# Last chunk of a gated feed-forward: half of its token tiles by seven products, the chunks of the second half in another order

## The chip, the core and the metric

The kernel runs on one core of one Trainium2 chip. The metric is the time of one execution in microseconds on the device; the time before is the median of three runs. One more execution was taken with the hardware profiler, and all rows below come from it. PE is TensorE (PEld its weight loads), DVE is VectorE, ACT is ScalarE, POOL is GpSimd, SP is SyncE, which issues the DMAs.

## What is computed

One block of a model on 2048 tokens of width 576: a layer norm, a linear attention with 32 heads, and a gated feed-forward of width 4608, all in float32.

```python
x = A_x                                        # [2048, 576]
xn = layernorm(x)
s = linear_attention(xn, A_wqkv, A_wo)         # phi(q) (phi(k)^T v) / (phi(q) . z), then @ wo
h = gelu(xn @ B_w1 + B_b1)                     # [2048, 4608]
g = silu(h @ B_w2 + B_b2)                      # [2048, 576]
return x + s * g
```

## The kernel before

**Precision.** TensorE works in a fast float32 form with a short mantissa. So each operand is split into a high part (ScalarE casts it, `set_hi`) and a low part (VectorE subtracts, `set_lo`), and each product is three matmuls: high by high, high by low, low by high. A split costs ScalarE one instruction and VectorE one, and the low one has two operands in SBUF.

**Stages.** The first 280 us compute the layer norm, the state of the attention and `s`, which is kept in DRAM (`s_dram`). The feed-forward follows: two halves of 1024 tokens, and in each half nine chunks (`NC`) of 512 hidden units (`CF` = 4 blocks of 128). A step of the loop is one chunk of one half: two up projections (`Up`, seven products each), then the down projection.

**Seven products.** Up and down projections are done by a Strassen-Winograd scheme: a two-by-two block product in seven block products instead of eight, with sums of operands ahead and sums of results behind. In the down projection the token side is split into two blocks of 512 tokens (b = 0, 1) and the output side into two halves of 288 columns. A token tile is 128 tokens; tiles 0 to 3 are block 0, tiles 4 to 7 block 1. `product(c, i, q2, ...)` does product i for two tiles (q2 and q2 + 1) of the block: 12 matmuls of 288 columns into one pair of PSUM banks (`bank2`, three pairs in rotation), after which VectorE adds the result into `macc` in SBUF (line 1293). Products 2, 3 and 4 add into the banks in which 1, 5 and 7 were formed (`CHAIN`), so they start only when VectorE has read those. `macc` holds C11, C12, C21, C22 and U1; U1 is added to the last three at the end (`combine`, line 1303). Sums of the gelu outputs are formed on GpSimd in place (`HOps.S`), sums of w2 likewise, and the split operands of both weights are stored in DRAM in the first half and loaded back in the second (`W1Loaded`, `W2.load`).

**Order.** Within a chunk VectorE, ScalarE, GpSimd and TensorE run in program order (`in_order`). What runs beside the 14 up products and 14 down products of a step is put at one of `NS` = 28 places by tables (`PH`, `PW2`, `W2_NEXT`), through `add(base + place, ...)`. The DMA queue of SP is ordered by the scheduler.

**The last step** (chunk 8 of the second half) does not use seven products for the down projection. `W2.plain` cuts the raw w2 chunk into four blocks, each split high and low; `tail_split` and `tail_lo` split the eight gelu outputs; `down_plain` does each of the eight token tiles by 24 matmuls of 288 columns and finishes it at once: VectorE adds the PSUM result to `macc` (line 1398), ScalarE applies silu (line 1399), VectorE multiplies by `s` (line 1356) and adds `x` (line 1357, for tile 6 on GpSimd), and the tile is written out (line 1358). Tile 7 is done in two column parts, 384 and 192, so that its end is short. `load_xs` brings the `x` and `s` tiles into buffers that have become free.

Of the kernel before, what the change touches and what calls it, by code (L numbers as in the profile page):

```python
# [44 lines left out]
def linear_attention_gated_ffn(ctx, tc, x, xT, wqkv, wo, w1, w1e, b1, w2, b2, out):  # L45
# [619 lines left out]

    def load_w2_raw(n):
        raw = w2rp.tile([P, 4, CF // 2, HD], F32, tag="w2raw", name=f"w2raw{n}")
        nc.sync.dma_start(raw.rearrange("p b a d -> p (b a d)"), w2[n % NC])
        return raw
# [155 lines left out]
    def load_we(n):  # L825

        we_sb[n] = w1p.tile([P, WB, P], F32R, tag="we", name=f"we_{n}", bufs=2)
        dst = we_sb[n].bitcast(F32).rearrange("p b c -> p (b c)")
        g, q = divmod(n % NP, WG)
# [8 lines left out]
    class W1:  # L838


        def __init__(self, n):
            self.n = n
            raw = stage_w1(f"w1raw{n}")
            nc.sync.dma_start(raw, w1[n % NP])
# [43 lines left out]
    class W1Loaded(W1):  # L888


        def __init__(self, n):
            self.n, self.tiles = n, {}
            for i in ("a", "c", "d"):
                if i == "c":
                    t = w1r.tile([P, 8, P], F32R, tag="stw", name=f"wc_{n}")
                else:
                    t = w1_tile(i, n)
                self.tiles[i] = t
                nc.sync.dma_start(t.bitcast(F32), w1_dram[n % NP, i])

    def load_six(n):

        t = w1_tile("e", n)
        for k in range(2):
            six[n + k] = t[:, 4 * k : 4 * k + 4]
            nc.sync.dma_start(six[n + k].bitcast(F32), w1_dram[(n + k) % NP, 6])
# [223 lines left out]
    class Up:  # L1130


        def __init__(self, n, w, xs):
            self.p, self.w = n % NP, w
# [54 lines left out]
    class W2:  # L1189


        def __init__(self, n):
            self.n, self.ops, self.tiles = n, {}, {}
# [14 lines left out]
        def plain(self, f):  # L1208
            k = 2 - 2 * (f % 2)
            self.src["p", f] = self.raw[:, k : k + 2, f // 2]  # L1210

        def hi(self, i):
            tag = ORDER[i[1]] if isinstance(i, tuple) else i
            self.tiles[i], self.ops[i] = op_tile(fr, [2, HD], f"w2_{tag}", 1, f"w2_{self.n}_")
            set_hi(self.ops[i], self.src[i])

        def lo(self, i):
            set_lo(self.ops[i], self.src[i], nc.vector)
            if self.n < NC - 1:
                keep_op(w2_dram, (self.n, i), self.tiles[i])  # L1220

        def load(self, i):
            t, self.ops[i] = op_tile(fr, [2, HD], f"w2_{i}", 1, f"w2_{self.n}_")
            nc.sync.dma_start(t.bitcast(F32), w2_dram[self.n % NC, i])

    class HOps:
# [10 lines left out]

        def S(self, i, pr):
            A = lambda r, c: self.A[pr, r, c]
# [11 lines left out]
            else:  # L1251
                src[7, pr] = mid[:, 3 + pr]
                tt(src[7, pr], A(0, 0), A(1, 0), op=SUB)  # L1253

        def hi(self, i, pr):
            self.ops[i, pr] = hi_lo(gp, [P, 512], f"h{HBUF[i, pr]}", 1, f"h{i}{pr}_")
            set_hi(self.ops[i, pr], self.src[i, pr])

        def lo(self, i, pr):
            set_lo(self.ops[i, pr], self.src[i, pr], nc.vector)  # L1260

# [48 lines left out]
    def load_xs(t):  # L1310
        F = lambda v: v.bitcast(F32)
        flat = lambda v: F(v).rearrange("p a b -> p (a b)")[:, :D]
        if t == 0:
            xt, s_t = flat(w1_tile("a", "x0")), stage_w1("s0")[:, :D]
        elif t == 1:
            xt = flat(w1_tile("a", "x1"))
            s_t = flat(w1p.tile([P, WB, P], F32R, tag="we", name="s1", bufs=2))
        elif t == 2:
            xt, s_t = (flat(w1_tile("a", f"{v}2")) for v in "xs")
        elif t == 3:  # L1320
            xt, s_t = stage_w1("x3")[:, :D], flat(w1_tile("a", "s3"))
        elif t == 4:
            raw = F(fr.tile([P, 2, D], F32R, tag="w2_5", name="xs4", bufs=1))
            xt, s_t = raw[:, 0], raw[:, 1]
        else:
            if t == 5:
                tails["h"] = F(x_hi(2, "xs56")).rearrange("p a b -> p (a b)")
                tails["l"] = F(x_lo(2, "xs7")).rearrange("p a b -> p (a b)")
            v = {5: tails["h"], 6: tails["h"][:, 2 * D :], 7: tails["l"]}[t]
# [5 lines left out]
    def tail_split(b, f):  # L1335
        src = h.A[f // 2, b, f % 2]
        if b == 0:
            pair = hi_lo(gp, [P, 512], f"h{f}", 1, f"hp{f}_")
        else:
            k = f % 2  # L1340
            if f < 2 and ("t", 0) not in tails:
                tails["t", 0] = x_lo(0, "hp0")
            if f >= 2 and ("t", 1) not in tails:
                tails["t", 1] = x_lo(1, "hp1")
            t = tails["t", f // 2]
            pair = t[:, 2 * k, :], t[:, 2 * k + 1, :]
        set_hi(pair, src)
        tails["hs", b, f] = pair, src

    def tail_lo(b, f):  # L1350
        pair, src = tails["hs", b, f]
        set_lo(pair, src, nc.vector)

    def gate(t, c, xt, s_t, cs=slice(0, D), eng=nc.vector):

        nc.vector.tensor_tensor(s_t[:, cs], c[:, cs], s_t[:, cs], op=MUL)
        eng.tensor_tensor(s_t[:, cs], s_t[:, cs], xt[:, cs], op=ADD)
        nc.sync.dma_start(out[t * P : (t + 1) * P, cs], s_t[:, cs])

# [27 lines left out]
    def down_plain(t, ws):  # L1387

        bi, q = divmod(t, QH)
        cs = slice(q * P, (q + 1) * P)  # L1390
        seq = []
        for f, (wh, wl) in enumerate(ws):
            hh, hl = tails["hs", bi, f][0]
            seq += [(hh, wh), (hh, wl), (hl, wh)]
        dst = c_tile(bi, q).rearrange("p n d -> p (n d)")

        def end(ps, c):
            nc.vector.tensor_tensor(c, ps, c, op=ADD)
            nc.scalar.activation(c, c, AF.Silu)

        def mm(ps, w, i):
            st, w_all = seq[i]
            nc.tensor.matmul(  # L1403
                ps, st[:, cs], w_all.rearrange("p n d -> p (n d)")[:, w],
                start=(i == 0), stop=(i == len(seq) - 1),
            )

        if t < 7:
            ps = bank2(f"pd{t}")
            for i in range(len(seq)):  # L1410
                for h in range(2):
                    mm(ps[:, h, :HD], slice(h * HD, (h + 1) * HD), i)
            end(ps[:, :, :HD], as2(dst))
            gate(t, dst, *tails["xs", t], eng=nc.gpsimd if t == 6 else nc.vector)
            return

        parts = [slice(0, 384), slice(384, D)]
        ps = []
        for k, w in enumerate(parts):
            n = w.stop - w.start  # L1420
            ps.append(bank1(f"pd{t}_{k}")[:, :n])
            for i in range(len(seq)):
                mm(ps[k], w, i)
        for k, w in enumerate(parts):
            end(ps[k], dst[:, w])
        for w in parts:
            gate(t, dst, *tails["xs", t], cs=w)
# [62 lines left out]
    )  # L1490
    plans = {}
# [20 lines left out]
    for step in range(n_chunks):  # L1512
# [3 lines left out]
        h = HOps(c)  # L1516
# [23 lines left out]
        elif not plain:  # L1540
# [3 lines left out]
            if step + 2 < n_chunks:  # L1544
                make(W2, w2t, step + 1)
                for i, at in W2_NEXT.items():
                    add(base + at + 10 * change, lambda i=i, n=step + 1: w2t[n].load(i))
            else:
                make(W2, w2t, step + 1)
                add(base + 7, w2t[step + 1].load_raw)  # L1550
        if not plain:
# [8 lines left out]
            for what in ("S", "hi", "lo"):  # L1560
                for (i, pr), at in PH[what].items():
                    add(base + at, getattr(h, what), i, pr)
        else:
            for f in range(CF):
                w2t[step].plain(f)
                add(base + (1, 2, 3, 8)[f], w2t[step].hi, ("p", f))
                add(base + (2, 3, 8, 9)[f], w2t[step].lo, ("p", f))
# [14 lines left out]
        if plain:  # L1582
            for m in (C12, C21, C22):
                add(base + 4, combine, m, nc.gpsimd)
            for t, at in enumerate((6, 7, 12, 13, 5, 12, 12, 12)):
                add(base + at, load_xs, t)
            for b, f, at, lo in (
                (0, 0, 7, 8), (0, 1, 8, 9), (1, 0, 10, 10), (1, 1, 10, 11), (0, 2, 11, 12),
                (0, 3, 12, 13), (1, 3, 13, 13), (1, 2, 13, 13),
            ):  # L1590
                add(base + at, tail_split, b, f)
                add(base + lo, tail_lo, b, f)
# [66 lines left out]
```

## Time and profile before

| | |
|---|---|
| median of 3 runs | 1098.09 us (1097.7 to 1098.24) |
| profiled execution | 1098.02 us |
| its span, first to last instruction | 1096.3 us |
| around the span | 1.7 us |
| instructions | 18084 |
| first matmul of the last down projection | 1065.1 us |

Rows of a timeline give the start and the duration in us, the engine, the line of the kernel, the operation, the tile written and the tiles read, the shape and the count of merged instructions; in brackets the idle time before it and who ended it. A matmul row lasts longer than its place in the stream, since matmuls overlap: the distance from one start to the next is what counts. Rows by line give the least, median and largest duration in ns. Rows of windows give the busy time of an engine, its instructions, the clock granted to TensorE (1.00 is full), the busy share of the DMA engines and GB/s.

### The profile page before, as it was taken

Reading aid. Unit: us, or ns where it says so; the run is one execution under the profiler, and the core shown is the slowest. Engines: PE = TensorE matmul, PEld = TensorE weight load, DVE = VectorE, ACT = ScalarE, POOL = GpSimd, SP = SyncE. Lnnn points to the kernel's source line nnn. Section 1 sums busy time; section 2 is a strip of 40 time slices with the busy share of each in tenths; the row PEclk is TensorE's granted clock in tenths of the full one; section 3 lists DMA queues with packets and bytes.
Section 4 is the critical chain, followed back from the end, with each engine's and each line's share of the span. In section 5 each row is a group of like instructions: output and inputs, shape, how many; then the busy total and the mean of one; then the engine's idle time right before and its main releaser. Section 6 shows DMA issues by size and latency. Waiting matters only on the chain.

```text
span 1096.3 us, 18084 instructions
## 1 busy us (share of the span) xinstructions
PE 1088.6 (99%) x6702; PEld 1008.5 (92%) x6702; DVE 825.6 (75%) x1132; ACT 490.9 (45%) x844; POOL 472.7 (43%) x403
## 2 busy tenths in 40 slices
PE   9999999999999999999999999999999999999998
PEld 8999989999898998989989989899898998998987
DVE  7785748888798888888888888667476584664856
ACT  6454655555545354454453544524224233242352
POOL 4667444323546446464555553424234143242340
PEclk9999999999999999999999999999999999999999
DMA  7999834675959559486585779978676676766352
GB/s 248 269 262 280 311 135 160 205 242 188 342 214 344 190 211 332 152 317 233 187 330 167 287 239 405 387 249 296 210 245 217 204 236 217 229 222 228 122 181 87
DMA packets 88400, 262.54 MB, mean 239 GB/s; under 512 B 11894, under 2 KB 24182, under 8 KB 85624
## 3 DMA queue, kind: packets, MB, share of 16 engines
q1 hardware_dynamic: 88312, 261.38, 70.1%
q8 instruction: 53, 0.87, 0.3%
q14 instruction: 35, 0.29, 0.1%
HBM read 164.24 MB, written 95.17 MB: 237 GB/s over the span
## 4 chain that ended last, share of the span: by engine, by line
PE 99%; DVE 1%; issue 0%; POOL 0%; ACT 0%; DVEq 0%; POOLq 0%
PE pm L1287 35%; PE a L1148 10%; PE e L1148 10%; PE zy L1148 10%; PE pk L313 6%; PE pq L313 5%; PE ps_s L789 5%; PE b L1148 5%; PE pv L313 4%; PE pd L1403 2%; PE ps_kva L382 1%; PE ptp L771 1%; PE ps_kw L708 1%; PE warm L361 0%; PE ps_kvb L382 0%
## 5 line engine op out<-in xcount | busy, mean ns | idle before, releaser
L1293 DVE TENSOR_TENSOR macc<-pm,macc 128x576 f32<-128x576 f32 x218 | 163.8, 752 | 51.9 <-PE pm L1287 50.3
L813 ACT CAST h_h<-g 128x512 fp32r<-128x512 f32 x204 | 121.7, 621 | 133.9 <-PE pm L1287 132.8
L816 DVE TENSOR_TENSOR h_l<-g,h_h 128x512 fp32r<-128x512 f32 x204 | 161.7, 800 | 0.0
L1253 POOL TENSOR_TENSOR mid<-g 128x512 f32<-128x512 f32 x34 | 44.0, 1293 | 105.4 <-ACT g L1156 105.4
L1247 POOL TENSOR_TENSOR g<-g 128x512 f32<-128x512 f32 x34 | 54.9, 1615 | 49.4 <-DVE h_l L816 28.4
L1156 ACT ACTIVATE g<-b,b1c 128x512 f32<-128x512 f32 x36 | 24.8, 689 | 101.9 <-DVE b L1174 101.9
L1165 ACT COPY mid<-a 128x512 f32<-128x512 f32 x36 | 21.1, 585 | 96.4 <-PE a L1148 96.4
L859 POOL TENSOR_TENSOR w1raw<-w1raw 128x256 f32<-128x256 f32 x18 | 13.3, 737 | 116.7 <-ACT h_h L813 68.2
L1168 DVE TENSOR_TENSOR mid<-b,mid 128x512 f32<-128x512 f32 x36 | 24.8, 690 | 46.3 <-PE b L1148 43.0
L1375 POOL TENSOR_TENSOR fin1l<-fin1h,fin1l 128x288 f32<-128x288 f32 x8 | 6.4, 806 | 119.6 <-DMA fin1l<-s_dram 62.9
L1250 POOL TENSOR_TENSOR g<-g 128x512 f32<-128x512 f32 x34 | 55.2, 1623 | 2.7
L1148 PE MATMUL a<-h0r,wa 128*128 128x512 f32 x144 | 50.4, 390 | 0.0
L1148 PE MATMUL a<-xh,wa 128*128 128x512 f32 x144 | 50.4, 390 | 0.0
L816 DVE TENSOR_TENSOR h_l<-mid,h_h 128x512 fp32r<-128x512 f32 x34 | 48.8, 1437 | 1.2
L1156 ACT ACTIVATE g<-e,b1c 128x512 f32<-128x512 f32 x36 | 24.8, 689 | 51.5 <-DVE e L1181 51.5
L754 POOL TENSOR_TENSOR pbuf<-phiq,den 128x576 f32<-128x576 f32 x16 | 19.4, 1214 | 63.9 <-DVE den L753 63.9
L1244 POOL TENSOR_TENSOR g<-g 128x512 f32<-128x512 f32 x34 | 44.2, 1299 | 2.7
L1181 DVE TENSOR_TENSOR e<-e,mid 128x512 f32<-128x512 f32 x36 | 24.8, 689 | 21.5 <-PE e L1148 21.5
L1171 DVE TENSOR_TENSOR mid<-zy,mid 128x512 f32<-128x512 f32 x36 | 24.9, 691 | 19.5 <-PE zy L1148 19.5
L313 PE MATMUL pk<-wkv_h,xh 128*128 128x288 f32 (+1 forms) x160 | 38.1, 320 | 0.5 <-DVE xh L245 0.5
L313 PE MATMUL pk<-wkv_l,xh 128*128 128x288 f32 (+1 forms) x160 | 38.2, 321 | 0.0
L1174 DVE TENSOR_TENSOR b<-e,mid 128x512 f32<-128x512 f32 x36 | 25.2, 699 | 17.2 <-PE e L1148 16.2
(857 smaller groups left out, 3644.4 us busy)
## 6 DMA issues: line engine op xcount, KB each, us to landing
we<-we_dram SPq DMA_DIRECT2D x36, 448.0 KB
w2raw<-w SPq DMA_DIRECT2D x10, 1152.0 KB
op<-w2o SPq DMA_DIRECT2D x18, 576.0 KB
w1raw<-w SPq DMA_DIRECT2D x18, 512.0 KB
op_a<-wa SPq DMA_DIRECT2D x18, 512.0 KB
op_c<-wc SPq DMA_DIRECT2D x18, 512.0 KB
op_d<-wd SPq DMA_DIRECT2D x18, 512.0 KB
wc<-op_c SPq DMA_DIRECT2D x18, 512.0 KB
```

Source lines behind the costliest of these rows:

```text
L313: nc.tensor.matmul(ps[:, h, : ws.stop - ws.start], st, w[:, k, ws], start=(begin and i == 0), stop=(end and i == len(seq) - 1), skip_group ...
L789: nc.tensor.matmul(ps[:, h, :HD], st[:, k, :], w[:, k, h * HD : (h + 1) * HD], start=(i == 0), stop=(i == len(seq) - 1),)
L813: nc.scalar.copy(pair[0], src)
L816: eng.tensor_tensor(pair[1], src, pair[0].bitcast(F32), op=SUB)
L1148: nc.tensor.matmul(ps, st, mv, start=first and n == 0, stop=n == len(seq) - 1, skip_group_check=True,)
L1156: nc.scalar.activation(g, ps, AF.Gelu_apprx_tanh, bias=b1c[:, f : f + 1])
L1244: tt(src[5, pr], A(1, 0), A(1, 1), op=ADD)
L1247: tt(src[6, pr], src[5, pr], A(0, 0), op=SUB)
L1250: tt(src[3, pr], A(0, 1), src[6, pr], op=SUB)
L1253: tt(src[7, pr], A(0, 0), A(1, 0), op=SUB)
L1287: nc.tensor.matmul(ps[:, q, :HD], hs[p][st][:, cs], m[:, p, :], start=(n == 0 and i not in CHAIN), stop=(n == 5), skip_group_check=True,)
L1293: nc.vector.tensor_tensor(dst, src, dst, op=ADD)
```

## The change

In the second half the chunks are taken in the order 8, 0, 1, ..., 7 (`chunk`, `pair`). So the step after the change of halves uses the w2 operands of the chunk before it, which are still in SBUF, and loads none; and the last step works on chunk 7, whose seven w2 operands lie in DRAM, where chunk 8 had its raw weights loaded and split. One more block of w2, B01, is loaded raw and split (`load_b01`, `place_b01`).

In the last step the down projection of tiles 0, 1, 4 and 5 goes by seven products (`seventh`), 12 matmuls each; tiles 2, 3, 6 and 7 stay plain (`plain_tile`), 24 matmuls each. TensorE's order is: product 1, tile 2, products 2, 6, 7, 5, 4, 3, tiles 3, 6, 7. The sums and splits for the products are made on the 256 columns that they need (`LastHOps`, `PLAST`); most of them stand in the tail itself, between the products. U1 is added in two parts: for the plain tiles at the start of the step, for the others between the products, on GpSimd. The gate additions of tiles 4, 5, 0, 1 and 6 are on GpSimd, those of 2, 3 and 7 on VectorE. In tile 7 the first 384 columns are now formed by matmuls of 288 and 96 columns, since its w2 operand comes in halves.

The core of the diff:

```diff
+    def chunk(step):
+        return step if step < NC else (step - 1) % NC
+    def pair(n):
+        return 2 * chunk(n // 2) + n % 2
...
-            nc.sync.dma_start(t.bitcast(F32), w2_dram[self.n % NC, i])
+            nc.sync.dma_start(t.bitcast(F32), w2_dram[chunk(self.n), i])
...
+    class LastHOps(HOps):
+        def cut(self, t):
+            return t[:, :256]
+        def add(self, pr, g):
+            super().add(pr, g)
+            if ("-", pr) in self.src:
+                self.src["-", pr] = self.A[pr, 1, 0][:, 256:]
+        def place(self, i, pr):
+            if i in (1, 2):
+                return super().place(i, pr)
...
+    PLAST = dict(
+        S={(7, 0): 7, (5, 0): 8, (6, 0): 9, (3, 0): 9, (7, 1): 13, (5, 1): 13},
+        hi={(1, 0): 7, (2, 0): 8, (7, 0): 9, (4, 0): 10, (1, 1): 11, (2, 1): 12},
+        lo={(1, 0): 8, (2, 0): 8, (7, 0): 9, (4, 0): 10, (1, 1): 12, (2, 1): 13},
+    )
...
-            if step + 2 < n_chunks:
-                make(W2, w2t, step + 1)
-                for i, at in W2_NEXT.items():
-                    add(base + at + 10 * change, lambda i=i, n=step + 1: w2t[n].load(i))
-            else:
-                make(W2, w2t, step + 1)
-                add(base + 7, w2t[step + 1].load_raw)
+            if change:
+                w2t[step + 1] = w2t[step]
+            else:
+                make(W2, w2t, step + 1)
+                for i, at in W2_NEXT.items():
+                    add(base + at, lambda i=i, n=step + 1: w2t[n].load(i))
+            if step + 2 == n_chunks:
+                add(base + 7, w2t[step + 1].load_b01)
...
             for m in (C12, C21, C22):
-                add(base + 4, combine, m, nc.gpsimd)
+                add(base + 4, combine, m, nc.gpsimd, slice(2, 4))
...
-    ws = [w2t[step].ops["p", f] for f in range(CF)]
-    for t in range(2 * QH):
-        down_plain(t, ws)
+    def seventh(i):
+        product(c, i, 0, [h.ops[i, 0], h.ops[i, 1]], w.ops[i], held)
+    def split(*keys):
+        for i, pr in keys:
+            h.hi(i, pr), h.lo(i, pr)
+    def end_plain(t, ps):
+        plain_add(ps, c_tile(*divmod(t, QH)))
+        silu(t)
+    def gate(t, eng):
+        gate_mul(t)
+        gate_add(t, eng)
+
+    seventh(1)
+    h.S(6, 1), h.S(3, 1)
+    split((6, 0), (6, 1))
+    ps = plain_tile(2, h, w)
+    split((7, 1), (5, 0))
+    end_plain(2, ps)
+    seventh(2)
+    split((5, 1), (4, 1))
+    gate(2, nc.vector)
+    seventh(6)
+    for m in (C12, C21):
+        combine(m, nc.gpsimd, first)
+    split((3, 0), (3, 1))
+    seventh(7)
+    seventh(5)
+    combine(C22, nc.gpsimd, first)
+    split(("-", 0), ("-", 1))
+    seventh(4)
+    silu(4), silu(5)
+    seventh(3)
+    silu(0), silu(1)
+    for t in (4, 5):
+        gate(t, nc.gpsimd)
+    ps = plain_tile(3, h, w)
+    for t in (0, 1):
+        gate(t, nc.gpsimd)
+    end_plain(3, ps)
+    ps = plain_tile(6, h, w)
+    gate(3, nc.vector)
+    end_plain(6, ps)
+    A, B = bank1("pd7_0"), bank1("pd7_1")
+    ranges = [(A[:, :HD], 0, slice(0, HD), True), (A[:, HD:384], 1, slice(0, n), False)]
+    plain_mm(7, h, w, ranges)
+    plain_mm(7, h, w, [(B[:, : D - 384], 1, slice(n, HD), True)])
+    gate(6, nc.gpsimd)
...
```

More of the change, by code (lines that the diff above doesn't have):

```diff
@@ L1133, in __init__ @@
         def __init__(self, n, w, xs):
-            self.p, self.w = n % NP, w
+            self.p, self.w = pair(n), w
             self.xb = xs
@@ L1206, in sum4, with load_b01, place_b01 @@
             nc.gpsimd.tensor_tensor(t, t, self.src[(7, 1)[k]], op=SUB)
-        def plain(self, f):
-            k = 2 - 2 * (f % 2)
-            self.src["p", f] = self.raw[:, k : k + 2, f // 2]
+        def load_b01(self):
+            raw = w2rp.tile([P, 4, CF // 2, HD], F32, tag="w2raw", name="b01")[:, 3]
+            nc.sync.dma_start(raw.rearrange("p a d -> p (a d)"), w2[chunk(self.n)][:, 3 * D :])
+            self.src["x"] = raw
+        def place_b01(self):
+            t = x_hi(2, "b01p").rearrange("p a b -> p (a b)")
+            self.ops["x"] = [
+                t[:, k * D : (k + 1) * D].rearrange("p (a d) -> p a d", d=HD) for k in range(2)
+            ]
         def hi(self, i):
-            tag = ORDER[i[1]] if isinstance(i, tuple) else i
-            self.tiles[i], self.ops[i] = op_tile(fr, [2, HD], f"w2_{tag}", 1, f"w2_{self.n}_")
+            if i == "x":
+                self.place_b01()
+            else:
+                self.tiles[i], self.ops[i] = op_tile(fr, [2, HD], f"w2_{i}", 1, f"w2_{self.n}_")
             set_hi(self.ops[i], self.src[i])
@@ L1218, in lo @@
             set_lo(self.ops[i], self.src[i], nc.vector)
-            if self.n < NC - 1:
+            if self.n < NC - 1 and i in self.tiles:
                 keep_op(w2_dram, (self.n, i), self.tiles[i])
@@ L1251, in S @@
             else:
[L1252 removed]
+                src[7, pr] = self.cut(mid[:, 3 + pr])
                 tt(src[7, pr], A(0, 0), A(1, 0), op=SUB)
+        def place(self, i, pr):
+            return hi_lo(gp, [P, 512], f"h{HBUF[i, pr]}", 1, f"h{i}{pr}_")
         def hi(self, i, pr):
[L1256 removed]
+            self.ops[i, pr] = self.place(i, pr)
             set_hi(self.ops[i, pr], self.src[i, pr])
@@ L1333, in load_xs, with gate_mul, gate_add, silu @@
         tails["xs", t] = xt, s_t
[L1335 to L1338, printed above, removed]
-        else:
[L1340 to L1354, printed above, removed]
+    def gate_mul(t, cs=slice(0, D)):
+        _, s_t = tails["xs", t]
+        c = c_tile(*divmod(t, QH)).rearrange("p n d -> p (n d)")
         nc.vector.tensor_tensor(s_t[:, cs], c[:, cs], s_t[:, cs], op=MUL)
+    def gate_add(t, eng, cs=slice(0, D)):
+        xt, s_t = tails["xs", t]
         eng.tensor_tensor(s_t[:, cs], s_t[:, cs], xt[:, cs], op=ADD)
         nc.sync.dma_start(out[t * P : (t + 1) * P, cs], s_t[:, cs])
+    def silu(t, cs=slice(0, D)):
+        c = c_tile(*divmod(t, QH)).rearrange("p n d -> p (n d)")[:, cs]
+        nc.scalar.activation(c, c, AF.Silu)
     def silu_first(s):
@@ L1384, in finish_tiles, with plain_mm @@
         return tiles
-    def down_plain(t, ws):
+    def plain_mm(t, h, w, ranges):
         bi, q = divmod(t, QH)
-        cs = slice(q * P, (q + 1) * P)
         seq = []
[L1392 to L1427, printed above, removed]
@@ new lines, in plain_mm @@
+        for f in range(CF):
+            pr, par = divmod(f, 2)
+            i = {(0, 0): 1, (0, 1): 2, (1, 1): 4, (1, 0): "-"}[bi, par]
+            cs = slice((q - 2) * P, (q - 1) * P) if i == "-" else slice(q * P, (q + 1) * P)
+            hh, hl = (v[:, cs] for v in h.ops[i, pr])
+            seq += [(hh, 0, pr, par), (hh, 1, pr, par), (hl, 0, pr, par)]
+        for n, (st, v, pr, par) in enumerate(seq):
+            for ps, half, cs, begins in ranges:
+                i = {(0, 0): 1, (1, 0): 2, (1, 1): 3, (0, 1): "x"}[par, half]
+                nc.tensor.matmul(
+                    ps, st, w.ops[i][v][:, pr, cs], start=(begins and n == 0), stop=(n == len(seq) - 1),
+                    skip_group_check=True,
+                )
@@ L1429, in x_operands, with plain_tile, plain_add @@
+    def plain_tile(t, h, w):
+        ps = bank2(f"pd{t}")
+        plain_mm(t, h, w, [(ps[:, k, :HD], k, slice(0, HD), True) for k in range(2)])
+        return ps[:, :, :HD]
+    def plain_add(ps, c):
+        nc.vector.tensor_tensor(c, ps, c, op=ADD)
     def x_operands(h0, l0, h1, l1, s1, s2, s4, rs):
@@ L1515, in linear_attention_gated_ffn @@
         plain = step == n_chunks - 1
-        h = HOps(c)
+        h = LastHOps(c) if plain else HOps(c)
         if half == 0:
@@ L1559, in linear_attention_gated_ffn @@
                     add(base + 26 + k, combine, C21, nc.gpsimd, slice(2 * k, 2 * k + 2))
[L1560 to L1567, printed above, removed]
+        for what in ("S", "hi", "lo"):
+            for (i, pr), at in (PLAST if plain else PH)[what].items():
+                add(base + at, getattr(h, what), i, pr)
         if half == 1 and c == 0:
```

80 lines of the change are left out of this document (51 added, 29 removed).

## The prediction

> **What bounds the kernel now.** I read the page first, then the waits of PE over the whole span, then the chain of waits.
>
> ```profile
> span 1096.3 us, 18084 instructions
> PE 1088.6 (99%) x6702; PEld 1008.5 (92%) x6702; DVE 825.6 (75%) x1132; ACT 490.9 (45%) x844; POOL 472.7 (43%) x403
> ...
> PE warm L361 <- POOL ident masks.py:199: 1.5, 1, 1.5
> PE pk L313 <- DVE xh L245: 0.5, 1, 0.5
> PE e L1148 <- DVE b L1174: 0.3, 1, 0.3
> ...
> 1019.97 22.41 PE pm L1287 x168
> 1061.81 1.89 PE e L1148 x7
> 1065.28 25.71 PE pd L1403 x192
> ```
>
> TensorE never waits between the projections and the last up product, where 0.3 us goes; the chain is a string of matmuls at their issue rate (22.41/168 = 0.133 us for 288 columns). So the reordered chunks cannot gain by themselves: what they remove is the load of seven operands at the change of halves, and that is hidden.
>
> ```profile
> 700.00:720.00 20.00, 20.00 (x130) 1.00 1.00 381
> 720.00:740.00 20.00, 20.00 (x119) 1.00 0.62 196
> ```
>
> These windows (PE busy, granted clock, DMA share) have the DMA engines full for 20 us and TensorE busy throughout. I cost that part at nothing. The w1 operands of pairs 16 and 17 are now read back a few us after they were stored; a store that lands late would stop the up products near 707, and as no row shows such a pair I leave up to 1 us for it in the range, not in the sum. Its other half, seven operand loads and a 288 KB piece in place of one 1152 KB load ahead of the last chunk, is what every second-half chunk has had already; if those loads were late the first product would wait, and no earlier chunk shows it. All that is left is the last 33 us.
>
> **TensorE's own work in the tail.**
>
> ```profile
> 1065.12 0.70 PE L1403 MATMUL pd<-w__11202,hp_h 128*128 128x288 f32 x4
> 1077.89 0.95 PE L1403 MATMUL pd<-w__11202,hp 128*128 128x288 f32 x6
> 1081.07 0.95 PE L1403 MATMUL pd<-w__11202,hp 128*128 128x288 f32 x6
> 1087.41 0.68 PE L1403 MATMUL pd<-w__11202,hp 128*128 128x384 f32 x3
> 1089.49 0.47 PE L1403 MATMUL pd<-w__11202,hp 128*128 128x192 f32 x3
> 1090.47 0.50 PE L1403 MATMUL pd<-w__11301,hp 128*128 128x192 f32 x3
> ```
>
> A plain tile is 24 matmuls from 1077.89 to 1081.07: 3.18 us, 0.132 each. Four tiles (0, 1, 4, 5) go from 96 matmuls to 7 x 12 = 84: minus 12 x 0.132 = 1.6 us. In the last tile a 384-column matmul (2.08/12 = 0.173) becomes one of 288 and one of 96. No row has 96 columns. From below, going down from 192 columns (0.98/9 = 0.109) at the slope between 288 and 384 gives 0.07; from above, the 288-column row gives 0.13. I take 0.109, because 192 columns already lie above that slope (it would give 0.09), as if a floor were reached. So 12 x (0.132 + 0.109 - 0.173) = plus 0.8 (0.3 to 1.1).
>
> The Trainium skill (TensorE: Matmul & The Clock Gate, "Back-to-back issue gap") gives N/2.4 + 2.5 ns for a warm matmul, 42 ns at 96 columns, by which the 0.8 us would be nothing. Its rule for a weight load in the section "LDWEIGHTS" (128 columns / 1.2, 107 ns) is the one that the 0.109 us row agrees with, since each matmul here loads its weights. By the first rule TensorE would end 0.8 us earlier, and the forecast would stand, since below VectorE sets the end.
>
> The 0.35 us wait of TensorE at 1061.46 comes from VectorE, which has two 128x576 splits ahead of the add that frees the bank:
>
> ```profile
> 1061.81 1.66 PE L1148 MATMUL e<-s4r,wc 128*128 128x512 f32 x6 [0.35 <-DVE b L1174]
> 1057.40 1.27 DVE L816 TENSOR_TENSOR w__11226<-w2raw,w__11226 128x576 fp32r<-128x576 f32 x1
> 1061.07 0.69 DVE L1174 TENSOR_TENSOR b<-e,mid 128x512 f32<-128x512 f32 x1
> ```
>
> The new queue has two 512-column splits and one of 256 there, and GpSimd adds half of each block instead of the whole; I let the wait go. Without new waits TensorE would end 1.6 - 0.8 + 0.35 = 1.15 us earlier.
>
> **The rule that speaks against the change.** More of the tail now lies on VectorE and GpSimd together: ten hi/lo pairs are split, four sums, three block adds and five gate additions run on GpSimd, four gate products on VectorE right behind one another. What happens when both work shows in every chunk:
>
> ```profile
> 1023.31 1.29 POOL L1244 TENSOR_TENSOR g<-g 128x512 f32<-128x512 f32 x1
> 1024.69 1.64 POOL L1247 TENSOR_TENSOR g<-g 128x512 f32<-128x512 f32 x1
> 1026.40 1.62 POOL L1250 TENSOR_TENSOR g<-g 128x512 f32<-128x512 f32 x1
> ...
> 1023.92 1.24 DVE L816 TENSOR_TENSOR h_l<-mid,h_h 128x512 fp32r<-128x512 f32 x1
> 1025.08 0.75 DVE L1293 TENSOR_TENSOR macc<-pm,macc 128x576 f32<-128x576 f32 x1
> 1025.75 1.12 DVE L816 TENSOR_TENSOR h_l<-g,h_h 128x512 fp32r<-128x512 f32 x1
> 1026.80 0.75 DVE L1293 TENSOR_TENSOR macc<-pm,macc 128x576 f32<-128x576 f32 x1
> 1027.46 1.11 DVE L816 TENSOR_TENSOR h_l<-g,h_h 128x512 fp32r<-128x512 f32 x1
> 1033.48 0.68 DVE L816 TENSOR_TENSOR h_l<-g,h_h 128x512 fp32r<-128x512 f32 x1
> ```
>
> Three splits end at 1025.16, 1026.87 and 1028.57: each 0.54 to 0.56 us after the end of the GpSimd instruction that ran when it began (1024.60, 1026.33, 1028.02), instead of lasting 0.68. The add that reads PSUM is not touched (0.75). So a VectorE instruction with two SBUF inputs waits until the running GpSimd instruction is through, then runs; the next GpSimd instruction waits for it in turn (1.62 instead of 1.29). They take turns by whole instructions. The Trainium skill (GPSIMD Engine Reference, "Specifications") says the SBUF interfaces are shared and that VectorE instructions with two SBUF inputs contend; the trace agrees, and adds the size.
>
> **The new wait.** Prices:
>
> ```profile
> 1090.02 1.42 POOL L1357 TENSOR_TENSOR xs<-xs 128x576 f32<-128x576 f32 x1 [31.96 <-DVE xs L1356]
> L859 POOL TENSOR_TENSOR w1raw<-w1raw x18: 732/737/743, 276.9 to 643.9; 128x256 f32<-128x256 f32 x18
> L862 POOL TENSOR_TENSOR w1t<-w1raw x18: 733/1105/1142, 277.8 to 644.7; 128x256 f32<-128x256 f32 x18
> L870 ACT CAST w<-w1t x18: 407/407/409, 278.5 to 645.9; 128x256 fp32r<-128x256 f32 x18
> 1066.24 0.68 ACT L1156 ACTIVATE g<-zy,b1c 128x512 f32<-128x512 f32 x1
> 1067.97 1.28 ACT L1399 ACT_TABLE_LOAD   x1
> 1076.41 0.76 DVE L1356 TENSOR_TENSOR wa_s<-macc,wa_s 128x576 f32<-128x576 f32 x1 [0.75 <-ACT macc L1399]
> 1077.20 0.76 DVE L1357 TENSOR_TENSOR wa_s<-wa_s,wa_x 128x576 f32<-128x576 f32 x1
> 1078.09 0.76 DVE L1398 TENSOR_TENSOR macc<-pd,macc 128x576 f32<-128x576 f32 x1
> 1091.88 0.56 DVE L1357 TENSOR_TENSOR xs<-xs 128x384 f32<-128x384 f32 x1
> 1092.36 0.35 DVE L1356 TENSOR_TENSOR xs<-macc,xs 128x192 f32<-128x192 f32 x1
> 1092.74 0.36 DVE L1357 TENSOR_TENSOR xs<-xs 128x192 f32<-128x192 f32 x1
> ```
>
> A 128x256 split on VectorE I estimate between the 192- and 384-column rows, 0.40. An instruction that needs the one before it on VectorE starts 0.79 after it (1076.41, 1077.20), one that doesn't 0.1 before its end (1026.80, 1027.46: 0.66). The tail begins at 1064.8 (1065.12 less the wait). TensorE, in the new order: product 1 to 1066.4, tile 2 to 1069.55, products 2, 6, 7, 5 to 1071.15, 1072.75, 1074.35, 1075.95. Product 4 adds into the bank of product 7, so it waits until VectorE has read that.
> VectorE's road there: the last gelu ends at about 1066.6; GpSimd's sums (7,1), (5,1), (6,1) at 0.74 and a gap each, one beside a split, end at 1069.1; ScalarE casts three halves and loads the silu table (1.28) to 1071.4, silu of tile 2 and two casts to 1073.0; VectorE's split of (4,1) ends at 1073.7. Then, in its order: gate of tile 2 (0.79 + 0.66), add of product 6 (0.67), a split (0.31): 1076.1. Now GpSimd, released by the add of product 6, is in the first block add (1.42, to 1077.4), and the next split has two SBUF inputs: it ends at 1077.7, the add of product 7 at 1078.45. TensorE starts product 4 at 1078.5 instead of 1075.95: plus 2.55 us (without turns 1.2; with GpSimd's sums at 1.1 about 3.3). Behind it nothing waits again: product 3 to 1081.65, tiles 3, 6 to 1088.0, tile 7 to 1092.2, against 1090.47 + 3 x 0.109 = 1090.8: plus 1.4.
>
> **The end of the tail is VectorE's.** The second split of "-" waits for the third block add (to 1080.9), the adds of products 4 and 3 end at 1082.6. Then four gate products in turn with four gate additions of GpSimd: the first two end at 1084.0, GpSimd at 1085.3, then 0.6 and 1.3 by turns: the fourth at 1087.8. Add of tile 3 to 1088.4, silu to 1089.2, its gate product behind a GpSimd addition to 1091.2, gate addition 1091.9. Add of tile 6, done by TensorE at 1088.0, only now: 1092.6; silu 1093.4, product 1094.15, both adds of tile 7 to 1094.9. GpSimd's addition of tile 6 (to 1095.6) holds the gate of tile 7: 1096.05, 1096.6, 1096.9, 1097.2. Before, that last instruction ended at 1092.74 + 0.36 = 1093.1. Behind it lie one write and the finish, unchanged.
>
> **Sum.** Minus 1.6, plus 0.8, minus 0.35, plus 2.55 on TensorE = 1.4; VectorE's distance behind TensorE's end grows from 2.3 to 5.0: 2.7. Together plus 4.1 us on the profiled execution, 1098.02 (span 1096.3 and 1.7 around it), which stands within 0.1 of the median 1098.09: 1102.1.
>
> **Rivals.** First, on the other side: the turns do not decide, because the instructions fall into each other's gaps (in my road the gate product of tile 3 and a GpSimd addition come within 0.1 us of each other, and in the tail of before GpSimd had one instruction only). With no turns the wait at product 4 is 1.2, so that TensorE ends 1.6 - 0.8 + 0.35 - 1.2 = 0.05 early, and VectorE keeps up: 1098.0. With half of the 4.1 it is 1100.1. Neither is slower than can be told. It decides if the block add begins after the split that I put behind it, that is from 0.3 us of drift. For it: the order of arrival is my reckoning; against: twelve GpSimd instructions stand in the tail's queue, and turns cost in every chunk. 0.22.
> Second: the wait at product 4 does not exist, since sums and table load are done earlier than I reckon by over 2 us; then TensorE ends 1.15 us early and VectorE is not behind: 1096.9. The chain of sum, cast, table load, silu speaks against it. 0.04.
> Third: GpSimd's 256-column sums take the 1.1 us of the L862 row, and its macc instructions, whose steps are longer, more than 1.42. The wait reaches 3.3 us (plus 0.75), and eight such instructions at 0.1 to 0.2 more each add 0.8 to 1.6: 1103.6 to 1104.5. 0.16.
>
> **Numbers.** Forecast 0.58, rivals 0.22, 0.04, 0.16. A gain over 0.2% (2.2 us, about what a measurement of this kernel can tell from no change) would need more than the 1.15 us that TensorE can give: 0.02. Within 0.2%: the first two rivals less that, 0.24. Slower: 0.74. The range leaves out the second rival, most of the first and the far end of the third: 1099.2 to 1104.0.
>
> **What would show it.** In the new profile: 84 "pm" matmuls between the plain tiles and 12 of 96 columns at about 0.11; no wait of e for b at 1061; a wait of TensorE of 2.5 us for VectorE's read of product 7's bank near 1076; gate products of 1.2 to 2.0 us between GpSimd additions of 1.9; the add of tile 6 three to four us after its last matmul; the chain's last 10 us on DVE, POOL and ACT. I am wrong if TensorE does not wait at product 4, or if gate products beside GpSimd last 0.76.

## The result, and the profile after

| | before | changed |
|---|---|---|
| median | 1098.09 us (6 runs, 1097.56 to 1098.46) | 1101.97 us (6 runs, 1101.41 to 1103.22) |
| ratio to before | | 1.0038, 95% interval 1.0025 to 1.0051 |
| profiled execution, its span | 1098.02, 1096.3 us | 1102.05, 1100.3 us |
| first matmul of the tail | 1065.12 | 1065.04 |
| last VectorE instruction ends | 1093.10 | 1097.57 |
| the tail, from the one to the other | 27.98 us | 32.53 us |

It is slower by 3.9 us, against 4.0 forecast from the median. The page of the changed kernel, span and busy times:

```profile
span 1100.3 us, 18121 instructions
...
PE 1087.5 (99%) x6702; PEld 1007.3 (92%) x6702; DVE 830.5 (75%) x1136; ACT 491.2 (45%) x849; POOL 486.2 (44%) x418
```

And its waits of TensorE over the whole span (us in total, times, longest):

```profile
PE pm L1340 <- DVE macc L1346: 2.4, 1, 2.4
PE warm L361 <- POOL ident masks.py:199: 1.5, 1, 1.5
PE pt0a L232 <- DVE xn L204: 0.6, 1, 0.6
PE pk L313 <- DVE xh L245: 0.5, 1, 0.5
```

TensorE is busy 1.1 us less, and the span is 4 us longer: the page alone says that the loss is not TensorE's work. The wait of e for b is gone from the list, and one of 2.4 us stands in its place. The timeline of TensorE at that wait and in tile 7:

```profile
1061.64 0.39 PE L1155 MATMUL a<-h0r,we 128*128 128x512 f32 x1
1061.87 0.62 PE L1155 MATMUL e<-s4r,wc 128*128 128x512 f32 x2
...
1065.04 0.42 PE L1340 MATMUL pm<-w__10956,h_h 128*128 128x288 f32 x2
...
1074.58 1.75 PE L1340 MATMUL pm<-w__11106,hp 128*128 128x288 f32 x12
1078.76 1.85 PE L1340 MATMUL pm<-w__11068,hp 128*128 128x288 f32 x12 [2.44 <-DVE macc L1346]
...
1088.37 0.30 PE L1442 MATMUL pd<-w__10956,hp 128*128 128x288 f32 x1
1088.51 0.21 PE L1442 MATMUL pd<-b01p,hp 128*128 128x96 f32 x1
...
1091.24 0.54 PE L1442 MATMUL pd<-b01p,hp 128*128 128x192 f32 x3
...
1092.29 0.50 PE L1442 MATMUL pd<-w__11138,hp 128*128 128x192 f32 x3
```

Product 4 starts at 1078.76, 2.44 us after product 5 is through (its row ends at 1076.33). Twelve pairs of 288 and 96 columns take 1091.24 - 1088.37 = 2.87 us, 0.239 a pair, so 0.107 for 96 columns. TensorE ends at 1092.29 + 3 x 0.109 = 1092.6. VectorE and GpSimd, from the read of product 7's bank on:

```profile
1076.09 1.95 DVE L823 TENSOR_TENSOR hp<-g,hp 128x256 fp32r<-128x256 f32 x2
...
1076.25 3.06 POOL L1356 TENSOR_TENSOR macc<-macc 128x576 f32<-128x576 f32 x2 [6.09 <-DVE macc L1346]
...
1077.96 1.61 DVE L1346 TENSOR_TENSOR macc<-pm,macc 128x576 f32<-128x576 f32 x2
...
1083.84 1.82 POOL L1394 TENSOR_TENSOR wa_s<-wa_s,wa_x 128x576 f32<-128x576 f32 x1 [2.65 <-DVE wa_s L1390]
...
1084.30 1.98 DVE L1390 TENSOR_TENSOR wa_s<-macc,wa_s 128x576 f32<-128x576 f32 x1
...
1085.63 1.94 POOL L1394 TENSOR_TENSOR xs_h<-xs_h 128x576 f32<-128x576 f32 x1
...
1086.21 1.97 DVE L1390 TENSOR_TENSOR xs_m<-macc,xs_m 128x576 f32<-128x576 f32 x1
...
1089.60 1.86 DVE L1390 TENSOR_TENSOR s<-macc,s 128x576 f32<-128x576 f32 x1 [0.75 <-ACT macc L1399]
...
1092.17 0.75 DVE L1453 TENSOR_TENSOR macc<-pd,macc 128x576 f32<-128x576 f32 x1
...
1097.21 0.36 DVE L1394 TENSOR_TENSOR xs_l<-xs_l 128x192 f32<-128x192 f32 x1
```

Two splits of 256 columns last 1.95 us instead of the 0.75 of two undisturbed ones, while two block additions of GpSimd run from 1076.25. The gate products of tiles 4 and 5 still last 0.76 and 0.75; those of tiles 0, 1 and 3 last 1.98, 1.97 and 1.86 beside GpSimd additions of 1.82, 1.94, 1.94 and 1.42. The add of tile 6 starts at 1092.17.

### The profile page after: what moved, and what is told of

Same layout as the page of the kernel before. It is cut to its first block, busy times and chain, and to the rows that moved or that the text cites. A ratio compares the mean times of both kernels' runs of the same rounds, so it can differ in the third digit from the quotient of the medians.

```text
span 1100.3 us, 18121 instructions
## 1 busy us (share of the span) xinstructions
PE 1087.5 (99%) x6702; PEld 1007.3 (92%) x6702; DVE 830.5 (75%) x1136; ACT 491.2 (45%) x849; POOL 486.2 (44%) x418
## 4 chain that ended last, share of the span: by engine, by line
PE 95%; DVE 2%; DMA 2%; ACT 1%; issue 0%; POOL 0%; SPq 0%; DVEq 0%; POOLq 0%; ACTq 0%
PE pm L1340 35%; PE a L1155 10%; PE zy L1155 10%; PE e L1155 10%; PE pk L313 6%; PE pq L313 5%; PE ps_s L796 5%; PE b L1155 5%; PE pv L313 4%; PE ps_kva L382 1%; PE ptp L778 1%; PE ps_kw L715 1%; DMA x<-x 1%; DMA w1u<-w1e 1%; DMA w<-wqkv 0%
## 5 line engine op out<-in xcount | busy, mean ns | idle before, releaser
L1346 DVE TENSOR_TENSOR macc<-pm,macc 128x576 f32<-128x576 f32 x225 | 168.9, 751 | 52.5 <-PE pm L1340 50.3
L820 ACT CAST h_h<-g 128x512 fp32r<-128x512 f32 x208 | 124.1, 621 | 134.0 <-PE pm L1340 132.9
L823 DVE TENSOR_TENSOR h_l<-g,h_h 128x512 fp32r<-128x512 f32 x208 | 164.3, 797 | 0.0
L1273 POOL TENSOR_TENSOR mid<-g 128x512 f32<-128x512 f32 (+1 forms) x36 | 45.3, 1259 | 117.4 <-ACT g L1163 117.4
L1267 POOL TENSOR_TENSOR g<-g 128x512 f32<-128x512 f32 (+1 forms) x36 | 56.4, 1566 | 51.5 <-DVE h_l L823 30.3
L1270 POOL TENSOR_TENSOR g<-g 128x512 f32<-128x512 f32 (+1 forms) x36 | 56.8, 1579 | 2.8
L1264 POOL TENSOR_TENSOR g<-g 128x512 f32<-128x512 f32 (+1 forms) x36 | 45.8, 1273 | 2.8
```

The lines of the kernel that those rows point to most:

```text
L820: nc.scalar.copy(pair[0], src)
L823: eng.tensor_tensor(pair[1], src, pair[0].bitcast(F32), op=SUB)
L1264: tt(src[5, pr], A(1, 0), A(1, 1), op=ADD)
L1267: tt(src[6, pr], src[5, pr], A(0, 0), op=SUB)
L1270: tt(src[3, pr], A(0, 1), src[6, pr], op=SUB)
L1346: nc.vector.tensor_tensor(dst, src, dst, op=ADD)
```

## The experiments

On the chips of these runs the times scatter: those of the kernel before alone run from 1097.8 to 1105.2 us. In nine of the eleven profiles below TensorE waits in the layer norm stage, ahead of anything that the change touches, for 0.2 to 5.4 us. So each tail is also read inside its own trace, from its first matmul to the end of VectorE's last instruction. The wait, in the profile with the longest one and in another profile of the same kernel (two halves, below):

```profile
PE pk L313 <- ACT xh L287: 5.4, 1, 5.4
```

```profile
PE pk L313 <- ACT xh L287: 1.0, 1, 1.0
```

These two executions took 1105.66 and 1098.12 us, and the tail was 26.69 us in both. The tail of the changed kernel was 32.53 and 32.55 us in the two profiles in which the clock held. So a difference of some tenths between tails can be read from one trace of each kernel. The medians tell only large differences apart: for the runs without block additions, with tile 3 moved, with gate additions on VectorE and with the bank of product 7 first, the interval meets that of the changed kernel.

| kernel | TensorE's waits in the tail, us | tail, us | median, of before beside it | ratio and interval |
|---|---|---|---|---|
| before | 0 | 27.98 | 1098.09 | 1 |
| changed | 2.4 | 32.53 | 1101.97, 1098.09 | 1.0038 (1.0025 to 1.0051) |
| order of chunks alone | 0 | 27.99 | 1099.46, 1100.13 | 0.9997 (0.9986 to 1.0009) |
| no block additions | 1.2 | 31.30 | 1104.49, 1100.13 | 1.0037 (1.0023 to 1.0050) |
| tile 3 between 5 and 4 | 0 | 32.82 | 1102.84, 1100.13 | 1.0029 (1.0015 to 1.0043) |
| gate additions on VectorE | 2.4 | 31.71 | 1106.35, 1100.13 | 1.0064 (1.0048 to 1.0080) |
| changed, second chip | 2.4 | 34.03 | 1107.63, 1102.28 | 1.0050 (1.0033 to 1.0067) |
| bank of product 7 first | 0.6 + 1.6 | 33.14 | 1108.44, 1102.28 | 1.0052 (1.0038 to 1.0067) |
| early splits | 0 | 28.40 | 1102.66, 1102.28 | 1.0008 (0.9992 to 1.0024) |
| two halves | 0 | 26.69 | 1103.91, 1102.28 | 1.0011 (0.9997 to 1.0025) |
| two halves, third chip | 0 | 26.69 | 1098.20, 1100.95 | 0.9988 (0.9969 to 1.0006) |
| changed, third chip | 2.4 | 32.55 | 1104.01, 1100.95 | 1.0037 (1.0020 to 1.0055) |
| longer wait | 4.3 | 35.69 | 1109.67, 1100.95 | 1.0090 (1.0055 to 1.0126) |

**The order of the chunks alone.** The kernel before with `chunk` and `pair`, `w2t[step + 1] = w2t[step]` at the change of halves, and the old plain tail.

> The kernel before with the new order of the chunks alone: the last step is the old one, all eight tiles plain. My theory (the order costs and gains nothing): 1098.1 us, within 0.3, TensorE busy throughout from the up products of the change of halves to the tail, and the 0.35 us wait at the last up product still there. Rival (the order carries part of the loss, because w1 operands are read back right after they were stored or the seven operand loads come late): 1099 to 1102, with a wait of TensorE between 700 and 760 us or in the last step.

From its waits of TensorE:

```profile
PE e L1154 <- DVE b L1180: 0.4, 1, 0.4
```

The tail is 27.99 us, the old wait is still there (0.4), TensorE waits nowhere else from the change of halves on, and the ratio is 1 within 0.14%. The reorder is free. This run still loads raw weights ahead of its last step; that the seven operand loads of the changed kernel come in time is shown by its own waits, in which TensorE has no wait between the first projections and product 4. So all of the loss is the tail's.

**The block additions left out.** The result then lacks U1 in three of the four blocks of tiles 0, 1, 4 and 5; the rest of the work is the same.

```diff
-    for m in (C12, C21):
-        combine(m, nc.gpsimd, first)
...
-    combine(C22, nc.gpsimd, first)
```

> The changed kernel with the three block additions of the tail (C12, C21, C22 plus U1 for tiles 0, 1, 4, 5) left out, so that GpSimd does nothing between 1070 and 1083 us. My theory (VectorE's splits wait for the running GpSimd instruction): the four splits there last about 0.4 each again, TensorE waits 1.2 us at product 4 instead of 2.44, and the end comes 1.3 us earlier: 1100.7. Rival (VectorE's queue is simply too long there, whatever GpSimd does): the wait stays at 2.4 and the time at 1102.0.

Timeline of VectorE and TensorE at the same place:

```profile
1079.45 0.75 DVE L823 TENSOR_TENSOR hp<-g,hp 128x256 fp32r<-128x256 f32 x2
1080.12 1.61 DVE L1346 TENSOR_TENSOR macc<-pm,macc 128x576 f32<-128x576 f32 x2
...
1080.93 1.33 PE L1340 MATMUL pm<-w__11068,hp 128*128 128x288 f32 x8 [1.24 <-DVE macc L1346]
...
1081.65 0.75 DVE L823 TENSOR_TENSOR hp<-g,hp 128x256 fp32r<-128x256 f32 x2
1082.82 0.76 DVE L1346 TENSOR_TENSOR macc<-pm,macc 128x576 f32<-128x576 f32 x1 [0.42 <-PE pm L1340]
```

The two splits take 0.75 instead of 1.95, and the wait 1.24 instead of 2.44: the 1.20 us is one and the same. The tail is 1.23 shorter. So half of the wait is the turns, and the other half VectorE's queue, as the first rival had priced it (1.2). The two splits of "-" behind it are shorter as well (0.75 instead of 1.99), but nothing is gained by that: VectorE then waits 0.42 and 0.83 us until TensorE is through with products 4 and 3. So TensorE is only just behind VectorE's queue here.

**Tile 3 between products 5 and 4.**

```diff
     split(("-", 0), ("-", 1))
+    ps = plain_tile(3, h, w)
     seventh(4)
     silu(4), silu(5)
+    end_plain(3, ps)
...
-    ps = plain_tile(3, h, w)
...
-    end_plain(3, ps)
```

> Plain tile 3 is taken between products 5 and 4, so that TensorE has 3.2 us of work while VectorE reads the bank of product 7. Theory A (from 1070 us on VectorE, not TensorE, sets the end; the split of the loss into 1.4 of TensorE and 2.7 of VectorE in my sum is only bookkeeping): the wait at product 4 is gone, TensorE ends 2.4 us earlier, and the time stays at 1102.0 to 1102.4. Theory B (the sum as I wrote it, TensorE's delay plus VectorE's distance behind it): 1099.6.

TensorE has no wait left in the tail and ends 25.1 us after the tail's begin instead of 27.6; the tail is 32.82 us, 0.3 longer. Theory A holds and B falls: TensorE's 2.4 us are worth nothing by themselves. VectorE's rows, from the first gate product that meets GpSimd to its last instruction:

```profile
1084.96 1.99 DVE L1390 TENSOR_TENSOR wa_s<-macc,wa_s 128x576 f32<-128x576 f32 x1
1086.87 1.97 DVE L1390 TENSOR_TENSOR xs_m<-macc,xs_m 128x576 f32<-128x576 f32 x1
1088.77 1.97 DVE L1390 TENSOR_TENSOR s<-macc,s 128x576 f32<-128x576 f32 x1
1090.77 1.83 DVE L1394 TENSOR_TENSOR s<-s,wa_x 128x576 f32<-128x576 f32 x1
1092.53 0.75 DVE L1453 TENSOR_TENSOR macc<-pd,macc 128x576 f32<-128x576 f32 x1
...
1097.58 0.36 DVE L1394 TENSOR_TENSOR xs_l<-xs_l 128x192 f32<-128x192 f32 x1
```

The addition of tile 3 now meets a GpSimd instruction too (1.83 instead of 0.76). Its gate product starts 0.9 earlier in the tail, since it no longer waits for silu behind the add of tile 3 (0.75 in the changed kernel); the two together leave some 0.3 more.

**The gate additions on VectorE.**

```diff
-    for t in (4, 5):
-        gate(t, nc.gpsimd)
+    gate_mul(4), gate_mul(5)
+    gate_add(4, nc.vector), gate_add(5, nc.vector)
```

and the same for tiles 0 and 1.

> The gate additions of tiles 4, 5, 0 and 1 go from GpSimd to VectorE, two products then two additions at a time. My theory (the turns cost more than the additions themselves): all gate products and additions last 0.76, 0.67 from one to the next, TensorE's wait at product 4 stays at 2.44, and the time falls by about 1.0 us to 1101.0. Rival (no turns decide; VectorE's amount of work sets the end): four additions more on VectorE, 4 x 0.67 = 2.7 us later, less what it idled: 1103.5 to 1104.7.

```profile
1085.34 0.75 DVE L1390 TENSOR_TENSOR wa_s<-macc,wa_s 128x576 f32<-128x576 f32 x1
1086.01 0.75 DVE L1390 TENSOR_TENSOR xs_m<-macc,xs_m 128x576 f32<-128x576 f32 x1
1086.68 0.75 DVE L1394 TENSOR_TENSOR wa_s<-wa_s,x 128x576 f32<-128x576 f32 x1
```

Four instructions more on VectorE, and the tail is 0.82 shorter (31.71): an addition costs VectorE 0.67 when it does it itself, and a product that meets one of GpSimd's lasts 1.2 longer (1.97 less 0.75). The wait at product 4 is still 2.44. The profiled execution took 1100.99, 1.06 less than the changed kernel's; 0.82 of that is the tail. The other five took 1103.6 to 1109.1, at a mean granted clock of 0.994 to 0.996 instead of 0.999, and no profile shows in which stage. So the gain is shown in the tail only; by the medians this kernel is no faster than the changed one.

**The changed kernel on another chip, and the read of product 7's bank moved ahead.**

> The changed kernel once more, on the same chip as the three below: 1102.0, and 32.5 us from the first matmul of the tail to the end of VectorE's last instruction (28.0 in the kernel before).

The same wait of 2.44 us, but a tail of 34.03: 1.5 more, which is the clock (last section).

```diff
+    seventh(7)
     for m in (C12, C21):
         combine(m, nc.gpsimd, first)
     split((3, 0), (3, 1))
-    seventh(7)
```

> In VectorE's queue the read of product 7's bank is put ahead of the splits for product 3. If VectorE's work sets the end, the wait of TensorE at product 4 falls from 2.44 to 0.7 but comes back as 1.7 at product 3, whose split operands are now behind, and the tail stays at 32.5 us or gets longer by up to 0.6: 1102.0 to 1102.6. If the wait at product 4 were a fault of its place in the queue alone, TensorE and the end would come 1.7 us earlier: 1100.3.

TensorE at products 4 and 3:

```profile
1083.82 1.85 PE L1340 MATMUL pm<-w__11068,hp 128*128 128x288 f32 x12 [0.56 <-DVE macc L1346]
1087.25 1.83 PE L1340 MATMUL pm<-w__11138,hp 128*128 128x288 f32 x12 [1.58 <-DVE macc L1346]
```

The wait only changes its place, 0.56 at product 4 and 1.58 at product 3, and the tail is 33.14. The place in the queue is not the fault; the queue is.

**Early splits, and two halves.** In both, the splits of products 5, 3 and "-" for the first pair stand behind (6, 0), in VectorE's idle time at 1068 (1.88 us in the changed kernel's trace), the others ahead of tile 2's add.

```diff
-    h.S(6, 1), h.S(3, 1)
-    split((6, 0), (6, 1))
-    ps = plain_tile(2, h, w)
-    split((7, 1), (5, 0))
-    end_plain(2, ps)
+    h.S(6, 1)
+    h.S(3, 1)
+    split((6, 0))
+    split((5, 0))
+    split((3, 0))
+    split(("-", 0))
+    split((6, 1))
+    ps2 = plain_tile(2, h, w)
+    split((7, 1))
     seventh(2)
-    split((5, 1), (4, 1))
-    gate(2, nc.vector)
+    split((5, 1))
+    split((4, 1))
+    split((3, 1))
+    split(("-", 1))
+    end_plain(2, ps2)
...
```

Behind that, block additions and gate additions are VectorE's in the first kernel. In the second, GpSimd does C12 after product 5's add, and the gate additions of tiles 2, 1 and 6 beside VectorE's adds from PSUM.

> Same products and tiles on TensorE, another order on VectorE: the splits whose data is there (products 5, 3 and '-' of the first pair) go into VectorE's idle 2 us at 1068, the others ahead of the add of tile 2, the gate additions and block additions all go to VectorE, and no instruction of GpSimd is left after 1070 us. If VectorE's queue with its turns is the whole cause, TensorE has no wait over 0.1 us in the tail and the tail falls from 32.5 to 28.4 us: 1098.0, about the time before, because VectorE now works without a gap and is 3.5 us behind TensorE. If the added work of the seven products itself were too much whatever the order, it stays above 1100.

> As the run with early splits, and three more edits: GpSimd gets one block addition and three gate additions back, each at a place where VectorE has only adds that read PSUM or is idle; tile 7 is done in two halves of 288 columns, which takes 12 matmuls of 96 columns away from TensorE (1.0 us); the two products of tile 7 come before its two additions. If instructions with a PSUM source take no turns, the tail is 26.9 us, 1.1 shorter than before, and the time 1096.7. If they do, the four GpSimd instructions cost 0.7 each: 1099 to 1100.

Without a wait of TensorE the tails are 28.40 and 26.69 us. In the second, the timeline shows two adds from PSUM beside GpSimd at nearly their old length (1.42, against 1.41 with GpSimd idle in the first kernel), and GpSimd's addition at 1.44:

```profile
1087.74 1.42 DVE L1346 TENSOR_TENSOR macc<-pm,macc 128x576 f32<-128x576 f32 x2
...
1087.96 1.44 POOL L1394 TENSOR_TENSOR s<-s,wa_x 128x576 f32<-128x576 f32 x1 [2.66 <-DVE s L1390]
```

So the seven products themselves are affordable; the order of VectorE's queue and the use of GpSimd together made the loss. Both runs change the two at once, so they do not show how much each is worth. And the gain is small: once product 5 is read, VectorE works to the end with no pause over 0.2 us. By their medians both are faster than the changed kernel on the same chip (1.0008 and 1.0011 of before, against 1.0050, and the intervals do not meet), but not told apart from the kernel before. The expected tails (28.4 and 26.9) were met; the expected times of 1098.0 and 1096.7 were not; the kernel before itself took 1102.28 on this chip.

> The version with early splits and tile 7 in two halves again, beside the changed kernel and the kernel before on one chip: its tail was 26.7 us against 28.0, so 1096.7 where the layer norm stage does not wait, 1.3 us under the kernel before on the same chip; no wait of TensorE in the tail, and so no loss of clock there.

The tail is 26.69 again, 1.3 us under before. The time is not told apart from the kernel before (0.9988, 0.9969 to 1.0006), and the 1096.7 was not reached: the lowest of twelve executions took 1097.53. A version that beats both has been shown in the tail, not in the time.

**The changed kernel on a third chip, and a longer wait.** In the last kernel the two splits of "-" stand ahead of the read of product 7's bank.

> The changed kernel, on the same chip. Two profiles of it had the same wait of 2.44 us at product 4, but one kept the clock of 1.00 behind it and the other fell to 0.50 for 3.5 us, and its tail was 34.0 instead of 32.5 us. If that is chance of where the wait lies, its time is 3.9 us over the kernel before in some executions and 5.4 in others; if it belongs to the chip, all lie at one of the two.

The tail is 32.55 us, and the clock behind the wait 1.00. So the loss of the clock does not belong to the kernel alone. Whether it is chance, the place of the wait in time or the chip stays open, since each chip gave one profile of this kernel.

```diff
-    for m in (C12, C21):
-        combine(m, nc.gpsimd, first)
-    split((3, 0), (3, 1))
+    combine(C12, nc.gpsimd, first)
+    combine(C21, nc.gpsimd, first)
+    split((3, 0))
+    split((3, 1))
+    split(("-", 0))
+    split(("-", 1))
     seventh(7)
     seventh(5)
     combine(C22, nc.gpsimd, first)
-    split(("-", 0), ("-", 1))
```

> The changed kernel with the two splits of '-' moved ahead of the read of product 7's bank in VectorE's queue: the wait of TensorE at product 4 grows from 2.44 to 4.4 us. VectorE's work is the same, but product 4 and 3 and their adds come 1.9 us later. If the clock stays at 1.00, the tail is 34.4 us and the time 1103.9; if a wait of this length always costs the clock, 12 to 15 matmuls behind it take 0.26 instead of 0.13, and the tail is 35.5 to 36.5 us. If only VectorE's amount of work counted, the tail would stay at 32.5.

TensorE at product 4:

```profile
1082.63 3.18 PE L1340 MATMUL pm<-w__11068,hp 128*128 128x288 f32 x12 [4.31 <-DVE macc L1346]
```

The wait is 4.3 us, the clock falls behind it, and the tail is 35.69: the case with the clock lost. Here TensorE does move the end, because VectorE's queue now waits for products 4 and 3 (2.48 and 0.76 us).

## Why the prediction was right

**The sum.** In the tail it gave 32.4 us (1064.8 to 1097.2), and 32.53 was measured. TensorE's part: 27.4 against 1092.6 - 1065.04 = 27.6; the wait 2.55 against 2.44, and without turns 1.2 against 1.24; the 96-column matmuls 0.109 against 0.107. VectorE's distance behind TensorE: 5.0, and 5.0 was measured. Gate products of 1.2 to 2.0 between additions of 1.9: three of 1.86 to 1.98, beside additions of 1.82, 1.94, 1.94 and 1.42. The add of tile 6 three to four us after its last matmul: 1092.17 against 1088.5.

**Outside the tail** three terms that the sum did not have nearly cancel, and that the total came so near is partly luck. The changed kernel's profiled execution began its last step 0.57 us later (first matmul at 1042.78 instead of 1042.21; its list of waits has 0.6 at pt0a). From there to the tail it took 22.26 us instead of 22.91: 0.65 less, where the list of waits had given 0.35 for the old wait. And from VectorE's last instruction to the end of the span it is 2.73 instead of 3.20, where I had "unchanged"; no run shows why.

**What was bookkeeping.** I added 1.4 of TensorE to 2.7 of VectorE as if each were a cause. Tile 3 between products 5 and 4 takes the first away, and nothing is gained. The 4.1 is the delay of one queue, VectorE's, counted at two places; the TensorE wait is its symptom in this kernel. That is not so for a later TensorE: with the clock lost or the wait at 4.3 us, VectorE waits for TensorE, and the end moves. My line "I am wrong if TensorE does not wait at product 4" was too strong: without that wait the time would have been the same.

**The chain.** I expected GpSimd on it. From 1070 us on its time shows there as VectorE's:

```profile
1083.63 0.51 DVE xs_h L1390
1084.14 0.16 issue
1084.30 1.13 DVE wa_s L1390
1085.43 0.78 issue
1086.21 1.97 DVE xs_m L1390
1088.18 0.68 DVE macc L1453
```

A turn is no semaphore wait. It is inside the duration of the waiting instruction, or stands as "issue"; only the comparison of durations by shape shows it.

**The rivals.** The first (turns do not decide) falls by the run without block additions and by the gate additions on VectorE, 1.23 and 0.82 us. The second (no wait) and the third (slower sums) fall by the changed kernel's own rows: the wait is there, and the sums last 0.74 to 0.96. A slip in the first rival's sum does not matter: 1.6 - 0.8 + 0.35 - 1.2 is 0.05 late, not early.

## What to carry to other kernels

Before fewer matmuls are bought with more sums, splits and adds, add up VectorE's instructions in that stage at their distance from one to the next, and count each GpSimd instruction beside two-SBUF work as VectorE's time too. Give GpSimd work only where VectorE reads PSUM or idles. Remove the wait that the profile shows in a trial before it is counted as a cause: if the end does not move, another queue sets it.

## What the runs showed of the hardware

**A wait of TensorE can cost its clock, but not each time.** The same wait of 2.44 us at product 4 left the granted clock at 1.00 in two of the three profiles of the changed kernel, and in that of the gate additions on VectorE; it was followed by half of it in the one on the second chip. Waits of 0.56, 1.24 and 1.58 us in the tail left it at 1.00. The row behind the wait on the second chip:

```profile
1083.46 2.89 PE L1340 MATMUL pm<-w__11068,hp 128*128 128x288 f32 x12 [2.44 <-DVE macc L1346]
```

Windows of that profile, and below of the longer wait (PE, PEld, DVE, ACT, POOL busy with counts, clock, DMA share, GB/s):

```profile
1080.00:1082.00 2.00, 1.02 (x8) 0.79 (x7) 2.00 (x4) 0.00 (x0) 1.05 (x1) 1.00 0.37 147
1082.00:1084.00 2.00, 0.54 (x4) 0.54 (x5) 1.90 (x3) 0.00 (x0) 2.00 (x2) 0.98 0.00 0
1084.00:1087.00 3.00, 3.00 (x14) 3.00 (x14) 2.70 (x4) 0.00 (x0) 1.53 (x2) 0.50 0.00 0
1087.00:1089.00 2.00, 2.00 (x16) 2.00 (x15) 0.74 (x2) 1.26 (x2) 0.00 (x0) 0.92 0.00 0
```

```profile
1079.00:1082.00 3.00, 0.00 (x0) 0.00 (x0) 3.00 (x4) 0.00 (x0) 2.29 (x2) 1.00 0.04 17
...
1083.00:1085.00 2.00, 2.00 (x10) 2.00 (x10) 0.44 (x1) 0.00 (x0) 1.41 (x1) 0.50 0.00 0
```

The half clock comes behind the wait, when TensorE works again, and lasts some 3.4 us (all of 1084 to 1087, and by the 0.98 and 0.92 an estimated 0.1 and 0.3 us on either side); it cost that tail 1.5 us. The Trainium skill (TensorE: Matmul & The Clock Gate, "Part 1: The HAM clock gate (the "warmup" mystery)") has the clock halved after an idle window of about 3.4 us, and the windows run freely, not from the kernel's start. The length of the half clock agrees with that, and windows that run freely would let the same wait cost the clock in one execution and not in another. But here a wait of 2.44 us, shorter than such a window, was enough in one of four profiles. So either a window need not be wholly idle or it is shorter than that; no run here shows which.

**What takes turns.** VectorE's adds from PSUM keep 0.67 us from one to the next beside a running GpSimd instruction. Gate products and splits, with both inputs in SBUF, wait for its end: the product that starts at 1084.30 ends at 1086.28, 0.62 us after GpSimd's addition (1085.66); undisturbed ones follow each other every 0.67 us.
